# Gated linear attention and MLP: decays counted from a chunk's first token, and the state's gate fetched from exp(L) by two small DMAs in place of matmuls

## The chip, the cores and the metric

The kernel runs on one core of a Trainium2 chip. The metric is the time of one execution on the device in microseconds (us), the median of several runs; lower is better. TensorE (PE in the profile) does the matmuls and transposes, with its weight loads shown apart as PEld; VectorE is DVE, ScalarE is ACT, GpSimd is POOL, and SyncE (SP) only issues DMAs, from a queue of its own that it works off in order.

## The reference

```python
# q, k, v, alpha: (B=4, H=8, S=768, D=48), alpha in [0.8, 1]; state: (B, H, D, D), zero at first
for t in range(S):
    state = alpha[:, :, t, :, None] * state + np.einsum('bhd,bhe->bhde', k[:, :, t], v[:, :, t])
    y[:, :, t] = np.einsum('bhd,bhde->bhe', q[:, :, t], state)
x = y.transpose(0, 2, 1, 3).reshape(B, S, H * D)             # (4, 768, 384)
mu  = np.mean(x, axis=-1, keepdims=True)
var = np.mean((x - mu) ** 2, axis=-1, keepdims=True)
xn  = (x - mu) / np.sqrt(var + 1e-06) * g_ln
out = x + np.maximum(xn @ w_ch1, 0.0) @ w_ch2                # 384 -> 1536 -> 384
```

All is float32, but the two weight matrices come as float64 and are rounded to float32 inside the kernel.

## The kernel before

The sequence is cut into 6 chunks of 128 tokens. For each chunk c and each of the 4 batches b the attention goes through six stages: `decays`, `turn`, `scores`, `attend`, `turn_x`, `update`. Batches are staggered by one stage: in a wave, batch b is at stage "wave minus b". The MLP of chunk c (`hidden` 12 times over all four batches, then `project` in thirds for each batch) is spread between the attention steps of chunk c + 1; the last chunk's MLP stands alone at the end. The source order is then put into one fixed instruction order per engine by the framework's scheduler, and each engine works off its own list in order, waiting on semaphores.

`decays` takes the logarithm of alpha on ACT into `la` (line 178), sums it along the tokens by one matmul with a triangular matrix (line 180, into the PSUM tile `lps`), and takes exp of plus and minus that sum L on ACT (`eq`, line 190, and `ek`, line 189). DVE multiplies q by `eq` and POOL multiplies k by `ek`, both into `qk`. L is counted from the middle of the chunk (token 63), so that the state's next value needs two factors per head dimension: the decay over the first half of a chunk and that over the second. Four matmuls per chunk and batch make these (lines 181 to 184): for each of the 4 pairs of heads, `la` is the stationary operand (128x128) and two columns of ones and zeros (`halves`) move. Their results lie behind L in the same `lps` tile, ACT takes their exp (`ge`, line 191), and POOL makes the gate and applies it to the state (lines 202 to 205): second half of the last chunk times first half of this one (`gt`), spread to the block diagonal (`gm`), times the state (`st`).

`update` (lines 269 to 283) adds k'v to the state: four matmuls into `sps`, then one DVE operation. `attend` of the next chunk reads `st` at line 240.

Every float32 matmul shows as two MATMUL rows and two LDWEIGHTS rows in the profile, so the four small matmuls of one chunk and batch are 8 rows.

The weights come in 12 pieces of 768 KB (`ws`, line 123), three in flight; DVE rounds each in seven operations (lines 135 to 144) in the first 108 us. The loads of the next chunk's alpha, k, q and v (`ra`, `rk`, `rq`, `rv`, line 90) and the stores of the output (line 310) are on the same SP queue.

Of the kernel before, what the change touches and what calls it, by code (L numbers as in the profile page):

```python
# [9 lines left out]
FP32 = mybir.dt.float32  # L10
# [7 lines left out]
STAGED = 3  # float64 pieces of the weights in flight  # L18
MID = 63  # the token of a chunk that decays are counted from
# [3 lines left out]
def kernel(  # L23
# [11 lines left out]
    """Gated linear attention in chunks of 128 tokens, then x + relu(LN(x) w1) w2.  # L35

    Within a chunk, L[t] is the sum of log(alpha) from the chunk's middle to t. With
    q' = q exp(L) and k' = k exp(-L), the chunk's own part of y is (q' k'^T, s <= t) v. The
    state is kept as of the chunk's middle, so that the part of earlier chunks is q' state,
    and the state's next value is (state + k'^T v) times the decay from middle to middle.  # L40
    alpha in [0.8, 1] keeps |L| under 14.5; float32 carries |L| up to 88, and scores with a
    key later than the query, which could overflow before that, are never copied.

    Heads go in pairs, at partitions 0 and 64 (rows past the head's D are zero), and a
    pair's state is block diagonal. The MLP of chunk c, on the 128 tokens of all batches,
    runs between the stages of the attention of chunk c + 1.

    Weights given in float64 arrive as their bits and are rounded to float32 here.
    """
    nc = tc.nc  # L50
# [15 lines left out]
    work = ctx.enter_context(tc.tile_pool(name="work", bufs=2))  # L66
    ps = ctx.enter_context(tc.tile_pool(name="ps", bufs=2, space=bass.MemoryType.PSUM))
# [4 lines left out]
    after, upto = r[:, None] > MID, r[None, :] >= r[:, None]  # L72
    tri_np = (after & upto).astype(np.float32) - (~after & ~upto).astype(np.float32)
    const_np = np.concatenate(
        [
            tri_np,
            np.eye(P, dtype=np.float32),
            upto.astype(np.float32),
            np.stack([r <= MID, r > MID, r < 64, r >= 64], 1).astype(np.float32),
        ],  # L80
        1,
    )
# [10 lines left out]
    consts = cpool.tile([P, 3 * P + 4], FP32, name="consts")  # L93
    nc.scalar.dma_start(consts, nc.inline_tensor(const_np, name="consts").ap())
    tri, ident, mask = (consts[:, i * P:(i + 1) * P] for i in range(3))
    mask = mask.bitcast(INT32)
    halves, own = consts[:, 3 * P:3 * P + 2], consts[:, 3 * P + 2:]
# [27 lines left out]
    def round_weights(i):  # L125
        """float64 bits (sign, 11 exponent, 52 mantissa) -> float32, in seven operations:
        2^20 1.m from the top 20 mantissa bits plus the low 32 as an integer, rounded once,
        times the signed power of two, whose exponent field is e - 896 (below 0: to zero).
        Integers that pass through float32 arithmetic there are multiples of 2^20: exact."""
# [28 lines left out]
    # Log decays and scaled q, k by token, one per batch, with the heads padded to 64.  # L158
    las = [cpool.tile([P, NP, 2, 64], FP32, name=f"la{b}") for b in range(B)]
    qks = [cpool.tile([P, 2, NP, 2, 64], FP32, name=f"qk{b}") for b in range(B)]  # L160
    sts = [cpool.tile([P, NP, 2, D], FP32, name=f"st{b}") for b in range(B)]
    for b in range(B):
        nc.vector.memset(las[b].rearrange("p a b c -> p (a b) c")[:, :, D:], 0.0)
        nc.vector.memset(qks[b].rearrange("p i a b c -> p (i a b) c")[:, :, D:], 0.0)

    # Scores, key by query; nothing is ever written where the key is later than the query.
# [7 lines left out]

    def decays(c, b):
        la = las[b].rearrange("p a b c -> p (a b) c")
        qk = qks[b].rearrange("p i a b c -> p i (a b) c")
        nc.scalar.activation(out=la[:, :, :D], in_=raws.pop(("a", c, b)), func=AFT.Ln)
        lps = ps.tile([P, 512], FP32, name="lps", tag="a", bufs=3)
        nc.tensor.matmul(lps[:, :DM], tri, la[:, :, :D], start=True, stop=True)  # L180
        for p in range(NP):
            nc.tensor.matmul(lps[:, DM + 2 * p:DM + 2 * p + 2],  # L182
                             las[b][:, p].rearrange("p a b -> p (a b)"), halves,
                             start=True, stop=True)
        lv = lps[:, :DM].rearrange("p (h d) -> p h d", d=D)
        ek = work.tile([P, H, D], FP32, name="ek", tag="ek")
        eq = work.tile([P, H, D], FP32, name="eq", tag="eq")
        ge = work.tile([P, NP, 2], FP32, name="ge", tag="ge", bufs=2 * B)
        nc.scalar.activation(out=ek, in_=lv, func=AFT.Exp, scale=-1.0)  # L189
        nc.scalar.activation(out=eq, in_=lv, func=AFT.Exp)  # L190
        nc.scalar.activation(
            out=ge, in_=lps[:, DM:DM + 2 * NP].rearrange("p (a b) -> p a b", b=2),
            func=AFT.Exp)
        nc.gpsimd.tensor_mul(qk[:, 1, :, :D], raws.pop(("k", c, b)), ek)  # L194
        nc.vector.tensor_mul(qk[:, 0, :, :D], raws.pop(("q", c, b)), eq)  # L195
        if c + 1 < NCB:
            load(c + 1, b)
        gate_of[c, b] = ge
        if c > 0:
            gt = work.tile([P, NP], FP32, name="gt", tag="gt")  # L200
            gm = work.tile([P, NP, 2], FP32, name="gm", tag="gm")
            nc.gpsimd.tensor_mul(gt, gate_of.pop((c - 1, b))[:, :, 1], ge[:, :, 0])
            nc.gpsimd.tensor_mul(gm, gt.unsqueeze(2).broadcast_to([P, NP, 2]),
                                 own.unsqueeze(1).broadcast_to([P, NP, 2]))
            nc.gpsimd.tensor_mul(sts[b], sts[b],
# [168 lines left out]
```

## Time and profile before

| | |
|---|---|
| times of three runs | 593.79, 599.22, 600.25 us; median 599.22 |
| span of the profiled execution | 593.7 us (0.1 us under the lowest of the three times) |
| PE busy | 570.7 us, 96% of the span, 2600 matmul rows |
| PEld, DVE, ACT, POOL busy | 368.8, 222.6, 92.0, 57.8 us |
| DMA | 33.64 MB, nearly all on SP's queue |

The profile is of one execution. Its span runs from the first to the last instruction; the lowest of the three times is all but the same, so what lies around the span is about 0.1 us. Busy time of PE holds overlapping passes: the busy time of a group is a little longer than the distance from its start to the start of the next group.

### The profile page before, as it was taken

How to read it: one execution, taken by the hardware profiler on the slowest of the kernel's cores; microseconds unless marked ns; L12 is line 12 of the kernel's file. 1: busy time of each engine (PE TensorE's matmuls, PEld its weight loads, DVE VectorE, ACT ScalarE, POOL GpSimd, SP SyncE). 2: the span in 40 equal slices, each digit the busy share in tenths (PEclk: the TensorE clock that was granted, in tenths of full speed). 3: DMA queues.
4: the chain of work that ended last, by engine and by line, in shares of the span. 5: the costliest groups of instructions: out<-in, count | busy, mean ns of one | idle time of the engine just before them, and what ended most of it. 6: DMA issues, size and time to landing. Idle time of an engine off the chain costs nothing.

```text
span 593.7 us, 6372 instructions
## 1 busy us (share of the span) xinstructions
PE 570.7 (96%) x2600; PEld 368.8 (62%) x2600; DVE 222.6 (37%) x365; ACT 92.0 (15%) x229; POOL 57.8 (10%) x90
## 2 busy tenths in 40 slices
PE   5976899999999999999999999999999999999997
PEld 4876654777656667756577665667765566654553
DVE  2887899533233232233332223332233331211000
ACT  3221121110032210032210022210011210001000
POOL 2101001110031100031100013010011110000000
PEclk9766699999999999999999999999999999999999
DMA  8673352111121100022101111000000000000000
GB/s 287 218 265 97 130 172 94 40 54 41 54 81 40 41 28 27 28 75 72 35 6 41 40 55 39 16 27 14 28 13 1 0 1 13 28 13 1 0 27 27
DMA packets 21885, 33.64 MB, mean 57 GB/s; under 512 B 2528, under 2 KB 18016, under 8 KB 21856
## 3 DMA queue, kind: packets, MB, share of 16 engines
q1 hardware_dynamic: 21312, 33.04, 16.9%
q8 instruction: 20, 0.33, 0.2%
q10 hardware_dynamic: 544, 0.20, 0.1%
q14 instruction: 9, 0.07, 0.0%
HBM read 28.51 MB, written 4.72 MB: 56 GB/s over the span
## 4 chain that ended last, share of the span: by engine, by line
PE 95%; DVE 3%; DMA 1%; ACT 1%; issue 0%; SPq 0%; ACTq 0%
PE hps L292 32%; PE ops L305 32%; PE yps L244 8%; PE aps L228 5%; PE tps L213 4%; PE lps L182 3%; PE yps L240 3%; PE sps L276 3%; PE lps L180 3%; PE xps L266 1%; DMA rq<-in_q_dram 1%; DMA ra<-in_alpha_dram 1%; DVE ob L309 0%; DVE xn L256 0%; DVE at L231 0%; DVE ws L143 0%
## 5 line engine op out<-in xcount | busy, mean ns | idle before, releaser
L305 PE MATMUL ops<-w,hT 128*128 128x384 f32 x576 | 198.7, 491 | 2.0 <-DVE ob L309 2.0
L292 PE MATMUL hps<-xT,w 128*128 128x512 f32 x432 | 197.8, 601 | 0.0
L305 PEld LDWEIGHTS ops<-w,hT 128*128 128x128 f32 x576 | 104.7, 190 | 65.4 <-DVE ob L309 3.8
L292 PEld LDWEIGHTS hps<-xT,w 128*128 128x128 f32 x432 | 78.3, 191 | 79.7 <-issue 77.2
L194 POOL TENSOR_TENSOR qk<-rk,ek 128x384 f32<-128x384 f32 x24 | 24.0, 1001 | 418.4 <-ACT ek L189 413.5
L244 PE MATMUL yps<-rv,at 128*128 128x48 f32 x384 | 58.5, 284 | 2.7 <-DVE st L281 2.6
L244 PEld LDWEIGHTS yps<-rv,at 128*128 128x128 f32 x384 | 54.9, 210 | 3.5 <-DVE st L281 2.8
L195 DVE TENSOR_TENSOR qk<-rq,eq 128x384 f32<-128x384 f32 x24 | 25.2, 1049 | 59.9 <-ACT eq L190 53.8
L297 DVE TENSOR_SCALAR hT<-hps 128x512 f32<-128x512 f32 x36 | 24.8, 690 | 56.3 <-PE hps L292 56.3
L295 ACT ACTIVATE hT<-hps 128x512 f32<-128x512 f32 x36 | 21.5, 598 | 156.1 <-PE hps L292 156.1
L250 DVE BATCH_NORM_STATS2 stats<-x 128x6 f32<-128x384 f32 x24 | 13.4, 560 | 74.7 <-ACT x L247 74.7
L247 ACT COPY x<-yps 128x384 f32<-128x384 f32 x24 | 11.5, 480 | 171.2 <-PE yps L244 171.2
L231 DVE COPY_PREDICATED at<-consts,aps 128x512 f32<-128x512 int32 x48 | 32.5, 718 | 13.5 <-PE aps L228 13.5
L228 PEld LDWEIGHTS aps<-qkT 48*128 48x128 f32 x384 | 26.9, 209 | 16.0 <-issue 9.2
L309 DVE TENSOR_TENSOR ob<-ops,x 128x384 f32<-128x384 f32 x24 | 13.4, 558 | 61.8 <-PE ops L305 61.8
L228 PE MATMUL aps<-qkT 48*128 48x128 f32 x384 | 32.2, 310 | 3.2 <-DVE qkT L218 3.2
L213 PEld LDWEIGHTS tps<-consts,qk 128*128 128x128 f32 x192 | 24.7, 154 | 13.7 <-issue 9.5
L182 PEld LDWEIGHTS lps<-consts,la 128*128 128x128 f32 x192 | 28.3, 212 | 7.9 <-issue 2.9
L240 PE MATMUL yps<-st,qkT 128*128 128x96 f32 x160 | 32.8, 286 | 0.0
L213 PE MATMUL tps<-consts,qk 128*128 128x128 f32 x192 | 29.2, 299 | 3.0 <-DVE qk L195 2.1
L240 PEld LDWEIGHTS yps<-st,qkT 128*128 128x128 f32 x160 | 25.6, 192 | 6.2 <-issue 3.8
L218 DVE COPY qkT<-tps 128x512 f32<-128x512 f32 x24 | 16.6, 690 | 32.0 <-PE tps L213 32.0
(38 smaller groups left out, 338.4 us busy)
## 6 DMA issues: line engine op xcount, KB each, us to landing
ws<-in_moe_w_ch_dram SPq DMA_DIRECT2D x12, 768.0 KB, 4.4
ra<-in_alpha_dram SPq DMA_DIRECT2D x24, 192.0 KB, 3.3
rk<-in_k_dram SPq DMA_DIRECT2D x24, 192.0 KB, 2.4
rq<-in_q_dram SPq DMA_DIRECT2D x24, 192.0 KB, 2.5
rv<-in_v_dram SPq DMA_DIRECT2D x24, 192.0 KB, 2.6
out_dram<-ob SPq DMA_DIRECT2D x24, 192.0 KB, 1.9
consts<-consts ACTq DMA_DIRECT2D x1, 194.0 KB, 3.5
g_col<-in_moe_g_ln_dram ACTq DMA_DIRECT2D x1, 1.5 KB, 3.7
```

What stands on the lines that cost most here:

```text
L182: nc.tensor.matmul(lps[:, DM + 2 * p:DM + 2 * p + 2], las[b][:, p].rearrange("p a b -> p (a b)"), halves, start=True, stop=True)
L194: nc.gpsimd.tensor_mul(qk[:, 1, :, :D], raws.pop(("k", c, b)), ek)
L195: nc.vector.tensor_mul(qk[:, 0, :, :D], raws.pop(("q", c, b)), eq)
L213: nc.tensor.transpose(tps[:, p], qks[b][:, i, p].rearrange("p a b -> p (a b)"), ident)
L228: nc.tensor.matmul(aps[i][:, p], qkT[rows, 1, p], qkT[rows, 0, p], start=True, stop=True)
L231: nc.vector.copy_predicated(out=at[:, i], data=aps[i], mask=mask.unsqueeze(1).broadcast_to([P, NP, P]))
L240: nc.tensor.matmul(yps[:, p].rearrange("p a b -> p (a b)"), qkT[:, 0, p], sts[b][:, p].rearrange("p a b -> p (a b)"), start=True, stop=False)
L244: nc.tensor.matmul(yps[:, p, i], at[:, i, p], vt[:, 2 * p + i], start=(c == 0), stop=(c == 0 or i == 1))
L292: nc.tensor.matmul(hps, w1[:, f, j * P:(j + 1) * P], xT_of[c][:, f], start=(f == 0), stop=(f == NF - 1))
L295: nc.scalar.activation(out=hT_of[c][:, j], in_=hps, func=AFT.Relu)
L297: nc.vector.tensor_scalar_max(hT_of[c][:, j], in0=hps, scalar1=0.0)
L305: nc.tensor.matmul(ops_of[b], hT_of[c][:, j, b], w2[:, j], start=(j == 0), stop=(j == NJ - 1))
```

## The change

L now counts from the chunk's first token: the triangular matrix is plain, and the same one serves as the mask of the scores. The state is kept as of the chunk's end, and its gate is exp(L) of the chunk's last token, which is the last row (partition 127) of `eq`. That row is copied to DRAM by one DMA (`row`, 1 x 512 elements of 4 bytes) and read back with one element per partition and pair of heads by a second one (`gate`, 128 x 4 elements); both stand on SP's queue, in `decays`, ahead of the next chunk's loads in the source. The four matmuls, the third exp on ACT (`ge`) and the product of two halves on POOL (`gt`) are gone. The spreading to the block diagonal (`gm`) and the multiplication of the state stand in `update` now, behind the addition, and no longer in the next chunk's `decays`. `eq` becomes one tile per batch with heads padded to 64 columns, and `la` a dense tile with two buffers. In the last chunk nothing of the gate is made.

```diff
-    tri_np = (after & upto).astype(np.float32) - (~after & ~upto).astype(np.float32)
+    upto = (r[None, :] >= r[:, None]).astype(np.float32)
...
-    las = [cpool.tile([P, NP, 2, 64], FP32, name=f"la{b}") for b in range(B)]
+    eqs = [cpool.tile([P, NP, 2, 64], FP32, name=f"eq{b}") for b in range(B)]
...
     def decays(c, b):
-        la = las[b].rearrange("p a b c -> p (a b) c")
         qk = qks[b].rearrange("p i a b c -> p i (a b) c")
-        nc.scalar.activation(out=la[:, :, :D], in_=raws.pop(("a", c, b)), func=AFT.Ln)
+        eq = eqs[b].rearrange("p a b c -> p (a b) c")[:, :, :D]
+        la = work.tile([P, H, D], FP32, name="la", tag="la")
+        nc.scalar.activation(out=la, in_=raws.pop(("a", c, b)), func=AFT.Ln)
         lps = ps.tile([P, 512], FP32, name="lps", tag="a", bufs=3)
-        nc.tensor.matmul(lps[:, :DM], tri, la[:, :, :D], start=True, stop=True)
-        for p in range(NP):
-            nc.tensor.matmul(lps[:, DM + 2 * p:DM + 2 * p + 2],
-                             las[b][:, p].rearrange("p a b -> p (a b)"), halves,
-                             start=True, stop=True)
+        nc.tensor.matmul(lps[:, :DM], tri, la, start=True, stop=True)
...
-        nc.scalar.activation(
-            out=ge, in_=lps[:, DM:DM + 2 * NP].rearrange("p (a b) -> p a b", b=2),
-            func=AFT.Exp)
         nc.gpsimd.tensor_mul(qk[:, 1, :, :D], raws.pop(("k", c, b)), ek)
         nc.vector.tensor_mul(qk[:, 0, :, :D], raws.pop(("q", c, b)), eq)
         if c + 1 < NCB:
+            row = dram.tile([1, NP, P], FP32, name="row", tag="row")
+            gate = work.tile([P, NP], FP32, name="gate", tag="gate", bufs=B)
+            nc.sync.dma_start(row, eqs[b][P - 1:P].rearrange("o a b c -> o a (b c)"))
+            with nc.allow_non_contiguous_dma(reason="one row to columns"):
+                nc.sync.dma_start(gate, row.rearrange("o a c -> c (o a)"))
+            gate_of[c, b] = gate
             load(c + 1, b)
-        gate_of[c, b] = ge
-        if c > 0:
-            gt = work.tile([P, NP], FP32, name="gt", tag="gt")
-            gm = work.tile([P, NP, 2], FP32, name="gm", tag="gm")
-            nc.gpsimd.tensor_mul(gt, gate_of.pop((c - 1, b))[:, :, 1], ge[:, :, 0])
-            nc.gpsimd.tensor_mul(gm, gt.unsqueeze(2).broadcast_to([P, NP, 2]),
-                                 own.unsqueeze(1).broadcast_to([P, NP, 2]))
-            nc.gpsimd.tensor_mul(sts[b], sts[b],
-                                 gm.unsqueeze(3).broadcast_to([P, NP, 2, D]))
...
     def update(c, b):
...
+        gm = work.tile([P, NP, 2], FP32, name="gm", tag="gm")
+        nc.gpsimd.tensor_mul(gm, gate_of.pop((c, b)).unsqueeze(2).broadcast_to([P, NP, 2]),
+                             own.unsqueeze(1).broadcast_to([P, NP, 2]))
         if c == 0:
             nc.vector.tensor_copy(out=sts[b], in_=sps)
         else:
             nc.vector.tensor_add(sts[b], sps, sts[b])
+        nc.gpsimd.tensor_mul(sts[b], sts[b],
+                             gm.unsqueeze(3).broadcast_to([P, NP, 2, D]))
```

The order on PE, at the start of chunk 2's attention, before (line 180 is the matmul for L, 182 the four small ones, 292 `hidden`, 213 the transposes of `turn`; the numbers at `la` and `qk` are buffers, one per batch):

```order
L180 MATMUL lps<-la_117,consts 128x384
L292 MATMUL hps<-xT,w_105 128x512 x3
L182 MATMUL lps<-consts,la_117 128x2 x4
L292 MATMUL hps<-xT,w_105 128x512 x3
L213 MATMUL tps<-consts,qk_121 128x128 x8
L292 MATMUL hps<-xT,w_105 128x512 x3
L180 MATMUL lps<-la_118,consts 128x384
L182 MATMUL lps<-consts,la_118 128x2 x4
L292 MATMUL hps<-xT,w_105 128x512 x3
```

The same place now (line 173 is the matmul for L, 278 `hidden`, 194 the transposes):

```order
L173 MATMUL lps<-la,consts 128x384
L278 MATMUL hps<-xT,w_107 128x512 x6
L194 MATMUL tps<-consts,qk_123 128x128 x8
L278 MATMUL hps<-xT,w_107 128x512 x3
L173 MATMUL lps<-la,consts 128x384
L278 MATMUL hps<-xT,w_107 128x512 x3
```

The 24 groups of four small matmuls are gone, and every other PE row stands where it stood, here and in the whole program.

On SP's queue, behind the first chunk's 16 loads, before:

```order
L123 DMA ws<-in_moe_w_ch_dram 128x3x256 x3
L90 DMA ra<-in_alpha_dram 128x384
L90 DMA rk<-in_k_dram 128x384
L90 DMA rq<-in_q_dram 128x384
L90 DMA rv<-in_v_dram 128x384
L90 DMA ra<-in_alpha_dram 128x384
L90 DMA rk<-in_k_dram 128x384
L90 DMA rq<-in_q_dram 128x384
L90 DMA rv<-in_v_dram 128x384
L123 DMA ws<-in_moe_w_ch_dram 128x3x256
```

The same place now (line 183 copies the row to DRAM, 185 fetches the gate; line 185 waits until the `row` of the same batch has landed):

```order
L115 DMA ws<-in_moe_w_ch_dram 128x3x256 x3
L183 DMA row<-eq_119 1x512
L83 DMA ra<-in_alpha_dram 128x384
L83 DMA rk<-in_k_dram 128x384
L83 DMA rq<-in_q_dram 128x384
L185 DMA gate<-row 128x4x1
L83 DMA rv<-in_v_dram 128x384
L183 DMA row<-eq_120 1x512
L83 DMA ra<-in_alpha_dram 128x384
L83 DMA rk<-in_k_dram 128x384
L83 DMA rq<-in_q_dram 128x384
L185 DMA gate<-row 128x4x1
```

Four small DMAs now stand ahead of the fourth weight load, and each `gate` has three loads between it and its `row`.

On POOL, from the last batch of chunk 1 to the first ones of chunk 2, before (line 194 multiplies k; `st_125` to `st_128` are the states of the four batches):

```order
L194 TENSOR_TENSOR qk_124<-rk,ek 128x8x48
L202 TENSOR_TENSOR gt<-ge 128x4
L203 TENSOR_TENSOR gm<-gt,consts 128x8
L205 TENSOR_TENSOR st_128<-st_128,gm 128x384
L194 TENSOR_TENSOR qk_121<-rk,ek 128x8x48
L202 TENSOR_TENSOR gt<-ge 128x4
L203 TENSOR_TENSOR gm<-gt,consts 128x8
L205 TENSOR_TENSOR st_125<-st_125,gm 128x384
```

The same place now (line 178 multiplies k, 262 spreads the gate, 268 multiplies the state; the states are `st_127` to `st_130`):

```order
L178 TENSOR_TENSOR qk_126<-rk,ek 128x8x48
L268 TENSOR_TENSOR st_127<-st_127,gm 128x384
L262 TENSOR_TENSOR gm<-gate,consts 128x8
L268 TENSOR_TENSOR st_128<-st_128,gm 128x384
L262 TENSOR_TENSOR gm<-gate,consts 128x8
L268 TENSOR_TENSOR st_129<-st_129,gm 128x384
L268 TENSOR_TENSOR st_130<-st_130,gm 128x384
L178 TENSOR_TENSOR qk_123<-rk,ek 128x8x48
```

The four state multiplications of a chunk now stand together, ahead of the first multiplication of k of the next chunk, and `gt` is gone.

## Rows read from the trace of the kernel before

**Rows 1.** The page: busy times, and the chain that ended last by engine and line.

```profile
PE 570.7 (96%) x2600; PEld 368.8 (62%) x2600; DVE 222.6 (37%) x365; ACT 92.0 (15%) x229; POOL 57.8 (10%) x90
...
PE 95%; DVE 3%; DMA 1%; ACT 1%; issue 0%; SPq 0%; ACTq 0%
```

**Rows 2.** Busy time of each engine by stretch (us), granted TensorE clock, DMA share, GB/s.

```profile
0.00:20.00 20.00, 13.17 (x62) 11.23 (x62) 7.19 (x16) 6.43 (x13) 4.04 (x8) 1.00 0.92 313
20.00:68.70 48.70, 38.00 (x195) 34.44 (x196) 41.42 (x67) 9.64 (x28) 4.91 (x6) 0.59 0.48 156
68.70:108.00 39.30, 39.30 (x130) 19.81 (x129) 38.91 (x61) 7.46 (x16) 4.55 (x5) 0.98 0.36 125
108.00:550.00 442.00, 442.00 (x2108) 282.77 (x2107) 131.47 (x218) 67.86 (x171) 44.33 (x72) 1.00 0.10 32
```

**Rows 3.** Line 182 alone by stretch: PE busy, PEld busy, clock, DMA share, GB/s.

```profile
0.00:62.00 62.00, 7.25 (x40) 8.34 (x40) 0.73 0.66 220
62.00:594.00 532.00, 18.04 (x152) 19.96 (x152) 0.99 0.12 38
```

**Rows 4.** PE in order of time, chunk 2: start, duration, line, tiles, count.

```profile
159.93 0.84 PE L180 MATMUL lps<-la,consts 128*128 128x384 f32 x2
160.60 2.74 PE L292 MATMUL hps<-xT,w 128*128 128x512 f32 x6
163.17 0.95 PE L182 MATMUL lps<-consts,la 128*128 128x2 f32 x8
163.98 2.82 PE L292 MATMUL hps<-xT,w 128*128 128x512 f32 x6
166.64 1.04 PE L213 MATMUL tps<-consts,qk 128*128 128x128 f32 x8
```

**Rows 5.** The chain that ended last, first 70 us: start, duration, what.

```profile
13.08 1.50 PE lps L182 x8
...
19.64 0.79 PE lps L182 x8
...
28.07 1.50 PE lps L182 x8
...
52.62 0.99 PE lps L182 x8
...
68.73 1.55 PE hps L292 x2
```

**Rows 6.** The first batch's `ek` and DVE's product of q and `eq`, in order of time.

```profile
7.80 0.49 ACT L189 ACTIVATE ek<-lps 128x384 f32<-128x384 f32 x1 [0.53 <-PE lps L182]
...
8.70 1.08 DVE L195 TENSOR_TENSOR qk<-rq,eq 128x384 f32<-128x384 f32 x1 [6.16 <-DMA ra<-in_alpha_dram]
```

**Rows 7.** Busy time by stretch of granted clock; columns as in rows 2.

```profile
18.70:22.10 3.40, 3.40 (x28) 3.08 (x29) 3.18 (x4) 0.97 (x4) 1.00 (x1) 1.00 1.07 374
22.10:39.20 17.10, 16.33 (x87) 14.81 (x88) 15.34 (x26) 5.48 (x15) 1.01 (x2) 0.50 0.52 171
56.30:69.90 13.60, 9.17 (x37) 8.28 (x38) 12.01 (x22) 0.97 (x3) 0.92 (x2) 0.50 0.43 134
```

**Rows 8.** DVE, emptying the tenth `hidden` result of chunk 0.

```profile
101.46 0.68 DVE L297 TENSOR_SCALAR hT<-hps 128x512 f32<-128x512 f32 x1
```

**Rows 9.** The page's DMA issues: queue, count, KB each, median us from issue to landing.

```profile
out_dram<-ob SPq DMA_DIRECT2D x24, 192.0 KB, 1.9
...
g_col<-in_moe_g_ln_dram ACTq DMA_DIRECT2D x1, 1.5 KB, 3.7
```

**Rows 10.** SP's queue in order of time: start, duration of the issue.

```profile
20.28 0.33 SPq L90 DMA_DIRECT2D rv<-in_v_dram  x1
27.40 0.38 SPq L123 DMA_DIRECT2D ws<-in_moe_w_ch_dram  x1
```

**Rows 11.** POOL: the product of k for chunk 1, batch 0; all multiplications of the state.

```profile
54.25 1.00 POOL L194 TENSOR_TENSOR qk<-rk,ek 128x384 f32<-128x384 f32 x1 [23.03 <-ACT ek L189]
...
L205 POOL TENSOR_TENSOR st<-st,gm 128x384 f32<-128x384 f32 x20 | 17.2, 860 | 1.6
```

More of the change, by code (lines that the diff above doesn't have):

```diff
@@ L18 @@
 STAGED = 3
-MID = 63
 @with_exitstack
@@ L66 @@
     work = ctx.enter_context(tc.tile_pool(name="work", bufs=2))
+    dram = ctx.enter_context(
+        tc.tile_pool(name="dram", bufs=B, space=bass.MemoryType.DRAM))
     ps = ctx.enter_context(tc.tile_pool(name="ps", bufs=2, space=bass.MemoryType.PSUM))
@@ L71 @@
     r = np.arange(P)
-    after, upto = r[:, None] > MID, r[None, :] >= r[:, None]
-    tri_np = (after & upto).astype(np.float32) - (~after & ~upto).astype(np.float32)
[L74 to L82, printed above, removed]
+    upto = (r[None, :] >= r[:, None]).astype(np.float32)
+    half = np.stack([r < 64, r >= 64], 1).astype(np.float32)
+    const_np = np.concatenate([upto, np.eye(P, dtype=np.float32), half], 1)
     raws = {}
@@ L91, in load @@
             raws[n, c, b] = t
-    consts = cpool.tile([P, 3 * P + 4], FP32, name="consts")
+    consts = cpool.tile([P, 2 * P + 2], FP32, name="consts")
     nc.scalar.dma_start(consts, nc.inline_tensor(const_np, name="consts").ap())
-    tri, ident, mask = (consts[:, i * P:(i + 1) * P] for i in range(3))
-    mask = mask.bitcast(INT32)
-    halves, own = consts[:, 3 * P:3 * P + 2], consts[:, 3 * P + 2:]
+    tri, ident, own = consts[:, :P], consts[:, P:2 * P], consts[:, 2 * P:]
+    mask = tri.bitcast(INT32)
     for b in range(B):
@@ L162 @@
     for b in range(B):
-        nc.vector.memset(las[b].rearrange("p a b c -> p (a b) c")[:, :, D:], 0.0)
+        nc.vector.memset(eqs[b].rearrange("p a b c -> p (a b) c")[:, :, D:], 0.0)
         nc.vector.memset(qks[b].rearrange("p i a b c -> p (i a b) c")[:, :, D:], 0.0)
@@ L175, in decays @@
     def decays(c, b):
-        la = las[b].rearrange("p a b c -> p (a b) c")
         qk = qks[b].rearrange("p i a b c -> p i (a b) c")
-        nc.scalar.activation(out=la[:, :, :D], in_=raws.pop(("a", c, b)), func=AFT.Ln)
+        eq = eqs[b].rearrange("p a b c -> p (a b) c")[:, :, :D]
+        la = work.tile([P, H, D], FP32, name="la", tag="la")
+        nc.scalar.activation(out=la, in_=raws.pop(("a", c, b)), func=AFT.Ln)
         lps = ps.tile([P, 512], FP32, name="lps", tag="a", bufs=3)
-        nc.tensor.matmul(lps[:, :DM], tri, la[:, :, :D], start=True, stop=True)
-        for p in range(NP):
-            nc.tensor.matmul(lps[:, DM + 2 * p:DM + 2 * p + 2],
-                             las[b][:, p].rearrange("p a b -> p (a b)"), halves,
-                             start=True, stop=True)
+        nc.tensor.matmul(lps[:, :DM], tri, la, start=True, stop=True)
         lv = lps[:, :DM].rearrange("p (h d) -> p h d", d=D)
         ek = work.tile([P, H, D], FP32, name="ek", tag="ek")
-        eq = work.tile([P, H, D], FP32, name="eq", tag="eq")
-        ge = work.tile([P, NP, 2], FP32, name="ge", tag="ge", bufs=2 * B)
         nc.scalar.activation(out=ek, in_=lv, func=AFT.Exp, scale=-1.0)
         nc.scalar.activation(out=eq, in_=lv, func=AFT.Exp)
-        nc.scalar.activation(
-            out=ge, in_=lps[:, DM:DM + 2 * NP].rearrange("p (a b) -> p a b", b=2),
-            func=AFT.Exp)
         nc.gpsimd.tensor_mul(qk[:, 1, :, :D], raws.pop(("k", c, b)), ek)
```

## The prediction

> **What bounds the kernel now.** I read the page first. PE is busy for 570.7 of 593.7 us, and the chain that ended last is PE for 95% of its length; DVE holds 3%, DMA and ACT 1% each, and POOL and SP next to nothing [rows 1]. So work taken off ACT, POOL or SP is worth nothing by itself, and work taken off PE should be worth its own length wherever PE never waits. The table by stretch says where that is [rows 2]. [...] From 68.7 to 108 us PE is busy throughout too, but so is DVE (38.91 of 39.30 us), which is rounding weights. From 20 to 68.7 us nobody is full: PE 38.00 and DVE 41.42 of 48.70 us, at a mean granted clock of 0.59. There the end is set by a chain that passes from PE to ACT to DVE and back, and I follow that chain instead of shares.
>
> **The four small matmuls (removed).** There are 24 groups of 8 rows on line 182, 192 rows: 40 rows (5 groups) before 62 us and 152 (19 groups) behind it [rows 3]. The new order takes out just these and moves no other PE row.
>
> The 19 late groups lie in a full PE. Their busy time is 18.04 us, or 0.95 us a group, but passes overlap, so this is the upper bound [rows 3]. The distance from the group's start to the next start, 163.17 to 163.98, is 0.81 us, which I use as the lower one [rows 4]. What comes behind counts too: six `hidden` rows take 2.57 us from start to start (160.60 to 163.17), and the six behind the group 2.66 (163.98 to 166.64), so the group costs 0.81 + 0.09 = 0.90 us [rows 4]. I take 0.88, the middle of the bounds and next to that figure. One group of the 19 (chunk 1, batch 1) lies in the stretch in which DVE is full. The tenth `hidden` result is emptied by DVE at 101.46 + 0.68 = 102.14 us [rows 8], and the twelfth needs its PSUM buffer; if PE arrives there earlier, it waits. I count that group as lost, which leaves 18 x 0.88 = 15.8 us (from 14.6 at 18 x 0.81 to 18.1 at 19 x 0.95).
>
> The 5 early groups lie on the chain. Four of its pieces are line 182: 1.50, 0.79, 1.50 and 0.99 us, 4.78 in all [rows 5]. The fifth group, the very first, holds `ek` until 7.80 us, and DVE's product starts at 8.70, right behind `eq`; I give it 1.50 us as well, the price of a group at the low rate [rows 5, 6]. That row names an alpha load as the releaser, but the product reads neither alpha nor what is loaded then; if it does wait on a load, these 1.50 us are nil. Of the piece at 28.07 I count only 0.3: from there to 52 us the chain runs through DVE's list, and DVE is busy for 85% of the stretch [rows 2, 5]. That makes 1.50 + 1.50 + 0.79 + 0.3 + 0.99 = 5.1 us (from 0 to 6.3).
>
> **The clock (a cost).** [...] `hidden` starts at 68.73 [rows 5], so now it runs 1.2 us at half rate, and loses 0.6. If it starts 5.1 us earlier and the clock still rises at 69.9, it runs 6.3 us at half rate and loses 3.1, 2.6 us more than now; if the rise moves along, nothing more. I take 0.9 us, nearer to the second, because the work that goes before the rise moves along as well.
>
> [...]
>
> **The two DMAs and the wait (added).** There are 20 pairs. Each `gate` waits on SP for its `row` to land; behind it on SP stand the next chunk's loads, in the first 108 us the weight loads, and later the output stores. The nearest row for a write to DRAM is the output store, 1.9 us to landing; for a fetch of single elements it is `g_col`, 384 elements, 3.7 us [rows 9]. With three loads issued in between, SP stands for a microsecond or two. In the first 20 us the queue is full (DMA share 0.92) and a `row` lies behind three pieces of 768 KB, some 7.5 us at 313 GB/s [rows 2, 9]. The cover is SP's own idle time: behind the eighth of the next loads at 20.28 it waits until 27.40 for DVE to free a weight buffer [rows 10]. From 108 us on the loads are for a chunk that begins tens of microseconds later. I put this at 0, from 0 to 3.7 us (one fetch laid open once); a gain is ruled out, since SP only gets more to do.
>
> [...]
>
> **ACT, POOL and the moved multiplication.** `ge` and `gt` go from engines that are not on the chain: 0. The state is multiplied in `update` now, 0.86 us each on POOL [rows 11], and the last of a chunk stands ahead of the next chunk's product of k. That product used to wait for `ek`, and `ek` for the small matmuls, which in chunk 2 begin 3.2 us behind the matmul for L (159.93 to 163.17) [rows 4]. `ek` can start some 3 us earlier, and the transposes that need the product come at 166.64, so 0.86 us is covered. `attend` reads the state a good part of a chunk later. Denser or padded tiles move the same elements: 0.
>
> **The sum.** 15.8 + 5.1 - 0.9 = 20.0 us. The profiled execution would come down from 593.8 to 573.8. It was the fastest of three; the other two are 5.4 and 6.5 us longer and nothing shows where. PE has no slack behind 108 us, so I place the difference ahead of that, leave it as it is, and apply the sum to the median: 599.2 - 20.0 = **579.2 us**. From the bounds the gain is 14.6 + 0 - 2.6 - 3.7 = 8.3 up to 18.1 + 6.3 = 24.4 us.
>
> **The rivals.** *The clock eats the early gain.* Fewer rows before 20 us could lose the full-rate stretch from 18.7 to 22.1: its 3.40 us of PE would take 6.8. With that and the 2.6 us, the early part is 5.1 - 3.4 - 2.6 = -0.9 us, the gain 14.9, the time 584.3. For it speaks that the clock sits at 0.50 for most of 22.1 to 69.9 [rows 7]; against it, that the chain here is partly DVE, which does not feel the clock.
>
> *DVE becomes the bound of the first 108 us.* Its idle time from 20 to 68.7 is 7.3 us, and from there to 108 it is 0.4 [rows 2]. If the order leaves DVE no way to close its gaps, the early part yields nothing and only the 18 groups count: 15.8 us, 583.4. Against it: one of its waits sits right behind the piece at 52.62 and should close with it.
>
> *The gate comes late.* POOL works in order, and the spreading of chunk 0's gates stands ahead of the product of k for chunk 1, batch 0, which started at 54.25 us [rows 11]. Chunk 0's last `eq` comes about 1 us behind 29.57, the end of the piece at 28.07 [rows 5]. So a gate has some 23 us to land; from there on each microsecond holds POOL. [...] Against it stands `g_col`, 3.7 us for three quarters of the elements.
>
> *The groups cost nothing in truth* (loads of weights hidden under the neighbours): then the time stays within 1%. The 0.81 us between starts in a full PE speaks against it [rows 4].
>
> **How the numbers follow.** Chances: the forecast 0.72; the early gain in full with a clock that moves along (24 us, 575) 0.07; clock 0.12; DVE 0.05; no gain 0.02; late gate 0.02. The range is 572 to 587: below by the full gains, above by the two rivals at 583 to 584 and an opened fetch of 3.7 us on top. A measurement here can tell about 1%, or 6 us, so faster has 0.95, the same 0.03, slower 0.02.
>
> **What would show it.** Of PE, no row of 128x2; PE full from about 103 us to the end of the attention, with each chunk 3.5 us shorter (4 x 0.88); `hidden` starting near 63.6 instead of 68.7; no wait of POOL on a DMA; `gate` landing in 3 to 6 us; the weights' last rounding on DVE no later than 106 us. Wrong would be: new PE idle time behind 108 us, `hidden` starting no earlier, or a weight load issued behind a `gate` that DVE then waits for.

## The result, and the profile after

| | before | after |
|---|---|---|
| median (us) | 599.31 | 575.82 |
| lowest to highest (four executions each) | 593.79 to 600.25 | 573.05 to 578.13 |
| span of the profiled execution | 593.7 | 576.1 |

The ratio is 0.9644, with a 95% interval from 0.9582 to 0.9707: 23.5 us less, where 20.0 was forecast. The four executions after fall into two pairs, 573.05 and 573.77, and 577.86 and 578.13; the median lies between them, where no execution was. Those before also spread, over 6 us. Much of what follows is about these two spreads.

One remark ahead corrects what stands above the prediction. The profiled execution after took 577.86 us with a span of 576.1, so 1.8 us lie around a span, and 598.96 against 597.2 in a later run of the kernel before says the same. The profiled execution before was therefore one of some 595.5 us. That its span lay 0.1 us under the lowest time was chance.

The page of the changed kernel, busy times and the chain that ended last; it answers to [rows 1].

```profile
PE 547.2 (95%) x2408; PEld 342.1 (59%) x2408; DVE 222.7 (39%) x365; ACT 90.2 (16%) x205; POOL 55.2 (10%) x70
...
PE 84%; DVE 9%; DMA 5%; SPq 1%; issue 0%; ACT 0%; ACTq 0%
```

PE has lost the 192 rows of the four small matmuls and 23.5 us of busy time. But the chain that ended last is no longer PE alone: 5% of it is now DMA. The table by stretch, with columns as in [rows 2], shows where time was won and lost.

```profile
20.00:62.00 42.00, 30.47 (x143) 26.32 (x142) 38.06 (x63) 7.38 (x20) 7.75 (x10) 0.58 0.59 174
62.00:68.70 6.70, 6.70 (x15) 3.04 (x15) 6.70 (x11) 0.60 (x1) 1.07 (x1) 0.82 0.40 141
68.70:108.00 39.30, 35.72 (x120) 18.19 (x118) 32.97 (x51) 6.73 (x13) 8.15 (x3) 0.96 0.34 110
108.00:550.00 442.00, 441.35 (x2002) 274.16 (x2002) 133.13 (x220) 68.11 (x157) 33.16 (x47) 1.00 0.11 32
```

From 108 us on PE is full but for 0.65 of 442 us. From 68.7 to 108 us, where PE and DVE had both been full, PE now idles for 3.6 us and DVE for 6.3.

PE in order of time, at the start of `hidden` (line 278), at the end of chunk 1's batch 1, and at the start of chunk 2; it answers to [rows 4] and the last of [rows 5].

```profile
62.07 11.66 PE L278 MATMUL hps<-xT,w 128*128 128x512 f32 x24
...
92.70 2.74 PE L278 MATMUL hps<-xT,w 128*128 128x512 f32 x6
99.03 4.28 PE L278 MATMUL hps<-xT,w 128*128 128x512 f32 x6 [3.58 <-DVE hT L283]
103.14 0.81 PE L173 MATMUL lps<-la,consts 128*128 128x384 f32 x2
...
156.62 0.84 PE L173 MATMUL lps<-la,consts 128*128 128x384 f32 x2
157.29 5.31 PE L278 MATMUL hps<-xT,w 128*128 128x512 f32 x12
162.44 1.04 PE L194 MATMUL tps<-consts,qk 128*128 128x128 f32 x8
```

The same landmarks before:

```profile
68.52 11.20 PE L292 MATMUL hps<-xT,w 128*128 128x512 f32 x24
...
99.59 5.45 PE L292 MATMUL hps<-xT,w 128*128 128x512 f32 x12
104.87 0.81 PE L180 MATMUL lps<-la,consts 128*128 128x384 f32 x2
```

I compare by these landmarks. The matmul for L of chunk 1, batch 2 starts at 103.14 us; before it started at 104.87. From there to the end of the span it is 473.0 us now (576.1 - 103.14) and was 488.8 (593.7 - 104.87). The difference is 15.87 us, where 18 groups at 0.88 make 15.84: the late term came out as forecast. `hidden` starts at 62.07 and not at 68.52, 6.45 us earlier, and the six rows at 92.70 start 6.89 us earlier (they were the first of the twelve at 99.59). Yet at 103.14 only 1.73 us of that are left. The rest went into two places that the rows show: a wait of 3.58 us for `hT`, and six `hidden` rows that take 4.28 us in place of 2.74.

The waits by who waited for whom (total, times, longest) name the new ones.

```profile
POOL gm L262 <- DMA gate<-row: 36.3, 8, 7.5
...
DVE w L127 <- DMA ws<-in_moe_w_ch_dram: 3.9, 1, 3.9
...
PE hps L278 <- DVE hT L283: 3.6, 1, 3.6
```

Followed back, the second and third are one event. Here are POOL, DVE and SP in order of time around it (start, duration, and what an idle time ended with).

```profile
80.54 0.68 DVE L283 TENSOR_SCALAR hT<-hps 128x512 f32<-128x512 f32 x1
81.06 6.83 POOL L178 TENSOR_TENSOR qk<-rk,ek 128x384 f32<-128x384 f32 x1 [17.04 <-ACT ek L176]
81.14 0.95 DVE L135 SCALAR_TENSOR_TENSOR ws<-ws 128x768 int32<-128x768 int32 x1
...
86.95 0.68 DVE L283 TENSOR_SCALAR hT<-hps 128x512 f32<-128x512 f32 x1
87.55 1.15 DVE L135 SCALAR_TENSOR_TENSOR ws<-ws 128x768 int32<-128x768 int32 x1
87.92 0.35 SPq L83 DMA_DIRECT2D rk<-in_k_dram  x1
...
88.85 0.38 SPq L115 DMA_DIRECT2D ws<-in_moe_w_ch_dram  x1
...
95.13 0.56 DVE L127 TENSOR_SCALAR w<-ws 128x768 int32<-128x768 int32 x1 [3.87 <-DMA ws<-in_moe_w_ch_dram]
...
98.29 0.68 DVE L283 TENSOR_SCALAR hT<-hps 128x512 f32<-128x512 f32 x1
```

POOL's product of k for chunk 1, batch 1 takes 6.83 us; the same product took 1.00 for batch 0 [rows 11]. The next load of k overwrites what this product reads, so SP stands until 87.92, and the last weight piece, queued behind, is issued at 88.85. DVE waits 3.87 us for it, until 95.13. DVE begins to empty the `hidden` result behind it in its order at 98.29, and PE has waited 3.58 us for that PSUM buffer.

The clock by stretch, columns as in [rows 7]:

```profile
13.60:23.80 10.20, 7.58 (x59) 5.68 (x56) 9.97 (x16) 3.69 (x9) 1.28 (x3) 0.98 0.85 292
...
37.40:64.70 27.30, 20.70 (x84) 16.91 (x83) 23.36 (x37) 3.12 (x9) 6.99 (x8) 0.51 0.52 155
64.70:98.80 34.10, 30.74 (x98) 14.56 (x96) 30.23 (x48) 6.04 (x11) 7.15 (x2) 1.00 0.37 119
98.80:102.20 3.40, 3.17 (x4) 1.47 (x5) 3.33 (x7) 0.00 (x0) 0.00 (x0) 0.54 0.00 0
```

The early stretch at the full rate, 3.4 us long in [rows 7], is now some 10 us long. (In the first 20 us the column alone does not tell the rate: it reads 1.00 in [rows 2] also where the 16 rows of batch 0's scores take 2.08 us, at 14.51 before. The scores of batch 1 take 1.16 us now, at 17.98, little more than half: that is the full rate, 1.16 us also at 85.48, where the clock is 1.00.) The last rise comes at 64.7 us, where before it came at 69.9: it moved along with the work. At the end of PE's wait the clock falls once more, from 98.8 to 102.2, and in that stretch lie the six rows that take 4.28 us.

The early part of SP's queue bears on the DMAs: the first `row` is issued at 11.22 us, and its `gate`, which waits for it, at 20.27.

```profile
11.22 0.31 SPq L183 DMA_DIRECT2D row<-eq  x1
...
20.27 0.38 SPq L185 DMA_DIRECT2D gate<-row  x1
...
23.35 0.38 SPq L185 DMA_DIRECT2D gate<-row  x1
24.38 0.38 SPq L115 DMA_DIRECT2D ws<-in_moe_w_ch_dram  x1
```

The chain that ended last even runs through the first two `row`s:

```profile
11.22 8.99 DMA row<-eq
...
21.29 2.05 DMA row<-eq
```

That alone does not price the DMAs, since another chain of the same length may stand beside it. Two of the experiments leave them out.

### The profile page after: what moved, and what is told of

The parts are those of the page before. It is cut to its first block, busy times and chain, and to the rows that moved or that the text cites. A ratio compares the mean times of both kernels' runs of the same rounds, so it can differ in the third digit from the quotient of the medians.

```text
span 576.1 us, 5992 instructions
## 1 busy us (share of the span) xinstructions
PE 547.2 (95%) x2408; PEld 342.1 (59%) x2408; DVE 222.7 (39%) x365; ACT 90.2 (16%) x205; POOL 55.2 (10%) x70
## 4 chain that ended last, share of the span: by engine, by line
PE 84%; DVE 9%; DMA 5%; SPq 1%; issue 0%; ACT 0%; ACTq 0%
PE ops L291 33%; PE hps L278 28%; PE yps L225 7%; PE aps L209 4%; PE yps L221 3%; PE tps L194 3%; PE sps L257 3%; PE lps L173 2%; DMA row<-eq 2%; DVE ws L135 1%; DVE w L129 1%; DMA rv<-in_v_dram 1%; PE xps L247 1%; DMA ws<-in_moe_w_ch_dram 1%; DVE w L136 1%; DVE ws L134 1%
## 5 line engine op out<-in xcount | busy, mean ns | idle before, releaser
L278 PEld LDWEIGHTS hps<-xT,w 128*128 128x128 f32 x432 | 80.4, 193 | 89.3 <-issue 78.3
L178 POOL TENSOR_TENSOR qk<-rk,ek 128x384 f32<-128x384 f32 x24 | 30.2, 1259 | 165.3 <-ACT ek L176 160.4
L268 POOL TENSOR_TENSOR st<-st,gm 128x384 f32<-128x384 f32 x20 | 18.1, 904 | 202.6 <-DVE st L267 181.3
L209 PE MATMUL aps<-qkT 48*128 48x128 f32 x384 | 31.0, 302 | 3.0 <-DVE qkT L199 3.0
L194 PEld LDWEIGHTS tps<-consts,qk 128*128 128x128 f32 x192 | 23.5, 148 | 16.4 <-issue 8.2
L194 PE MATMUL tps<-consts,qk 128*128 128x128 f32 x192 | 27.6, 286 | 4.9 <-DVE qk L179 4.2
```

The costliest lines, as they stand in the source:

```text
L194: nc.tensor.transpose(tps[:, p], qks[b][:, i, p].rearrange("p a b -> p (a b)"), ident)
L209: nc.tensor.matmul(aps[i][:, p], qkT[rows, 1, p], qkT[rows, 0, p], start=True, stop=True)
L268: nc.gpsimd.tensor_mul(sts[b], sts[b], gm.unsqueeze(3).broadcast_to([P, NP, 2, D]))
L278: nc.tensor.matmul(hps, w1[:, f, j * P:(j + 1) * P], xT_of[c][:, f], start=(f == 0), stop=(f == NF - 1))
```

## The experiments

**The changed kernel again**, beside the next three, to have more of its executions.

> The changed kernel once more, beside the others on one chip. Two things are in its first profile that the prediction did not have: the weight load that DVE waits for (3.9 us, from 91.3 to 95.1 us) and the 3.6 us for which PE then waits. If the chain behind it is fixed by the order of instructions (POOL's product of k for chunk 1, batch 1 lasts 6.8 us beside a gapless DVE, and the loads behind it on SP wait), the wait is in every profile and the times spread as before, 573 to 578 us. If it is a matter of luck, this profile is without it and about 5 us shorter.

It measured 576.27 us, with executions of 572.75, 573.73, 578.82 and 579.39; ratio 0.9654 (0.9582 to 0.9726). The profiled one (578.82) has the long product of k (6.70 us at 82.11), a wait of DVE for a weight piece (3.7) and of PE for `hT` (3.3). So the late weight load comes back. Of eight executions of this kernel four are at about 573 and four at 578 to 579.

**The small matmuls back, late and early.** The same matmuls stand again behind the one for L, once for chunks 2 to 5 (16 groups) and once for chunks 0 and 1 (8 groups). Their results are read by nobody.

```diff
         nc.tensor.matmul(lps[:, :DM], tri, la, start=True, stop=True)
+        if c >= 2:      # the other version: c < 2
+            for p in range(NP):
+                f = p % NF
+                nc.tensor.matmul(lps[:, DM + 2 * p:DM + 2 * p + 2],
+                                 la.rearrange("p h d -> p (h d)")[:, f * P:(f + 1) * P],
+                                 own, start=True, stop=True)
```

> The changed kernel with the four small matmuls put back in chunks 2 to 5 (16 groups), their result read by nobody; the gate still comes by the DMAs. If the groups cost PE their own time in a full PE, 16 x 0.88 = 14.1 us come back: about 590 us, and the stretch ahead of 108 us looks as in the changed kernel. If the gain came from the rest of the change (POOL, ACT, the moved multiplication), the time stays at 576 us; if the matmuls' cost was partly hidden weight loading, it lands between, near 583 us.

592.27 us, ratio 0.9895 (0.9856 to 0.9935). Its ten executions are three at 587.0 to 588.2 and seven at 591.5 to 594.0. The mean of the lower ones (587.75) stands 14.5 us above that of the changed kernel's two lower ones just above (573.24), and the mean of the higher ones (592.91) 13.8 above that of its two higher ones (579.11). That makes 0.86 to 0.91 us for each of 16 groups. The trace says the same: from the matmul for L of chunk 1, batch 2 to the end of the span it takes 487.2 us (589.7 - 102.48), 14.3 more than without the groups, or 0.89 each. They are paid in full.

> The changed kernel with the four small matmuls put back in chunks 0 and 1 alone (8 groups), their result read by nobody. On the chain of the first 60 us they cost 4.8 to 6.3 us, so the first hidden row starts near 68 us again and not at 62; the three groups of chunk 1 behind that cost up to 2.6 us, less what DVE's wait for the weights hides. If the early gain is real: 576 + 5 to 8 us, about 582. If, in addition, the late weight load is a consequence of the earlier exp (DVE has no gap left when POOL wants its operands), that wait is gone here, 5 us come back, and the time is about 577 to 579 us with the first hidden row late and no wait of DVE on weights. If the early groups were hidden: 576 us and nothing moves.

583.16 us (579.86, 580.92, 585.39, 586.85), ratio 0.9773 (0.9701 to 0.9845): 6.9 us above the changed kernel by the medians, 7.2 and 7.0 by the means of the lower and the higher pairs. `hidden` starts at 70.14 us, where the profiles of the kernel before have 68.52 and, below, 70.88 and 71.10. The weight load is late here too: the product of k lasts 6.49 us at 89.48, DVE waits 3.2 us. I had thought that the weight load is late because the earlier exp moved POOL's product of k forward into DVE's full stretch. With the early matmuls back that cannot be, and the theory fell.

**No DMAs**, the gate a constant 0.01:

```diff
...
+    ones = cpool.tile([P, NP], FP32, name="ones")
+    nc.vector.memset(ones, 0.01)
...
-            row = dram.tile([1, NP, P], FP32, name="row", tag="row")
...
-                nc.sync.dma_start(gate, row.rearrange("o a c -> c (o a)"))
-            gate_of[c, b] = gate
+            gate_of[c, b] = ones
```

> The changed kernel without the two DMAs: the gate is a constant, so the decay from chunk to chunk is left out; all other work stays. If the pairs of DMAs are free, as forecast, the time is that of the changed kernel (576 us, within 2 us). If SP's waiting for each row holds up the weights, or POOL's waiting for a gate delays anything, it is 3 to 6 us faster and the wait of DVE on the weight load is gone. If that wait comes from POOL's slow product of k alone, it stays, with the same 3.9 us.

573.07 us (572.84, 573.00, 573.14 and one of 579.41), ratio 0.9636 (0.9555 to 0.9717). By the text above this looks as if the DMAs cost 3 us, since the wait is gone too. The version with a constant gate and four pieces, below, shows that they do not. In the profiled execution (573.14) the product of k is short. POOL and DVE in order of time:

```profile
81.20 1.00 POOL L178 TENSOR_TENSOR qk<-rk,ek 128x384 f32<-128x384 f32 x1 [16.54 <-ACT ek L176]
...
81.29 1.72 DVE L133 SCALAR_TENSOR_TENSOR ws<-ws 128x768 int32<-128x768 int32 x1
```

Here POOL starts 0.09 us ahead of DVE's rounding step with two inputs, and it is that step which is held (1.72 us, normally 0.95). With the DMAs, in the first profile of the changed kernel, POOL started 0.08 ahead of that step and lost all the same; in the second POOL started at 82.11, 0.06 behind. In the other profiles that have the step beside it POOL won where it started 0.52 us ahead (four pieces, below), and lost where it started 0.19 to 0.28 behind (early matmuls; the two versions below with a late copy and with a constant gate and four pieces) and once with 0.03 ahead (late matmuls). So it looks like a race between two starts that are mostly 0.03 to 0.3 us apart, in part perhaps closer than the profile's times can order. The DMAs do not decide it alone: one execution without them took 579.41 us, which by its time belongs to the upper group, though it was not profiled. Whether they make the late load more frequent, four executions against eight can't tell.

**A fourth weight piece in flight**, so that the last pieces are issued before that product can hold them.

```diff
-STAGED = 3
+STAGED = 4
```

> The changed kernel with four pieces of the weights in flight in place of three. The last weight load then stands ahead of the next chunk's k load of batch 1 on SP's queue, so POOL's late product can't hold it up; PE, DVE and POOL keep their order. If the two levels of the times (573 and 579 us) come from this one load, all runs lie at the lower level: about 573 us, spread under 2 us, no wait of DVE on a weight load, PE not waiting near 95 us. If the levels come from the clock or from something else of the first 60 us, both stay, and the median is 576 us again.

573.09 us, six executions from 572.76 to 573.90, ratio 0.9595 (0.9559 to 0.9632). The upper group is gone. No wait for a weight piece is left, and the matmul for L of chunk 1, batch 2 starts 6.68 us earlier than before (104.87), not 1.73:

```profile
62.36 10.99 PE L278 MATMUL hps<-xT,w 128*128 128x512 f32 x24
...
98.19 0.81 PE L173 MATMUL lps<-la,consts 128*128 128x384 f32 x2
```

**That one product of k on DVE**, with three pieces:

```diff
-        nc.gpsimd.tensor_mul(qk[:, 1, :, :D], raws.pop(("k", c, b)), ek)
+        mul_k = nc.vector.tensor_mul if (c, b) == (1, 1) else nc.gpsimd.tensor_mul
+        mul_k(qk[:, 1, :, :D], raws.pop(("k", c, b)), ek)
```

> The changed kernel with the product of k for chunk 1, batch 1 alone on DVE in place of POOL: one instruction of 0.55 us more for DVE, and POOL not in the way. If POOL stands still for 6.8 us because DVE, busy without a gap, keeps it from its operands, the load behind it on SP goes out some 5 us earlier, DVE waits for no weights, and the time is 572 to 574 us in all runs. If POOL was slow for a reason of its own (its order, its gate), the k load is late again and the times keep both levels, 576 us in the median.

572.76 us (572.58 to 573.93), ratio 0.9591 (0.9546 to 0.9637). The weight piece is issued at 84.22 us and not at 88.85, and no one waits for it. Two different edits, one on the product and one on the queue behind it, remove the same group of executions.

**That product later**, by a small copy ahead of it on POOL:

```diff
+        if (c, b) == (1, 1):
+            late = work.tile([P, 64], FP32, name="late", tag="late", bufs=1)
+            nc.gpsimd.tensor_copy(out=late, in_=ek.rearrange("p h d -> p (h d)")[:, :64])
```

> The changed kernel with one small copy on POOL (64 columns of exp of minus L) ahead of the product of k for chunk 1, batch 1, so that this product starts a few tenths of a microsecond later. It is meant to lose a race: where POOL's start and the start of DVE's two-input rounding step lie within 0.1 us of each other, the one that comes first makes the other wait. If so, POOL's product lasts 6 to 7 us in every run, the last weight load is late, and all times are at the upper level, 578 to 580 us. If the levels have another source, the times keep both levels, 573 and 579 us.

579.29 us, three executions at 579.1 to 579.6 and one at 572.51; ratio 0.9661 (0.9594 to 0.9729). So not all executions are at the upper level, as I expected, and it was not the product that suffered. In order of time, POOL and the DVE operation at which it was let go:

```profile
82.40 5.81 POOL L180 COPY late<-ek 128x64 f32<-128x64 f32 x1 [17.31 <-ACT ek L176]
...
88.03 0.68 DVE L286 TENSOR_SCALAR hT<-hps 128x512 f32<-128x512 f32 x1
88.17 1.00 POOL L181 TENSOR_TENSOR qk<-rk,ek 128x384 f32<-128x384 f32 x1
```

A copy of 64 columns took 5.81 us, and the product behind it 1.00. So the length is not set by POOL's operation. In all six profiles with a held operation, what POOL starts there lasts until DVE has come to its next operation that reads PSUM.

**The kernel before with four pieces**: the edit of the fourth piece alone.

> The kernel before with four pieces of the weights in flight. Its times have two levels as well, 594 to 596 and 598 to 600 us. If these are the same late weight load, all runs come down to the lower level, about 594 us, and the whole of the change is then worth 594 - 573 = 21 us, level against level. If the upper level of the kernel before has another source (the clock in the first 70 us), both levels stay: 598 us in the median.

596.05 us, ten executions from 594.09 to 599.03, ratio 0.9977 (0.9943 to 1.0011): no change that can be told. The spread of the kernel before is not from a late weight piece: the profiled execution is the longest of the ten (599.03 us), and in it the product of k takes 1.01 us.

**The kernel before, one profile more.**

> The kernel before, one profile more. If its upper level (598 to 600 us) comes from the early chain and the granted clock, as the version of before with four pieces of weights suggests, a profiled execution of about 598 us or more shows hidden starting 1 us or more behind 68.7 us, a clock of 0.50 until some 5 us behind 69.9 us, and the distance from the first matmul for L of chunk 2 to the end unchanged, within 1 us, against the profile shown of before. If instead the late weight load (the k product on POOL beside a full DVE) makes it, hidden starts at 68.7, the product of k for chunk 1, batch 1 lasts over 5 us and not 1.00, and DVE waits for a weight piece. An execution near 594 us tells nothing and should repeat the rows shown.

This execution took 598.96 us, at the upper end. PE and the clock in it (order of time; stretches):

```profile
71.10 12.13 PE L292 MATMUL hps<-xT,w 128*128 128x512 f32 x24
```

```profile
69.90:74.80 4.90, 4.90 (x12) 2.79 (x12) 4.90 (x9) 0.00 (x0) 0.00 (x0) 0.54 0.64 202
74.80:108.00 33.20, 33.20 (x110) 16.32 (x109) 32.05 (x50) 6.10 (x12) 3.68 (x4) 1.00 0.35 119
```

`hidden` starts 2.6 us later than in the first profile (68.52) and the clock rises at 74.8 us, not 69.9; the first 24 rows take 12.13 us, where they took 11.20. Together that is 3.5 us, the whole difference of the spans (597.2 and 593.7). The product of k is short (1.00 us at 91.35). So what the prediction could not place lies early, in the chain and the clock ahead of `hidden` and just behind its start. Most of the 2.6 us have a place: the clock's mean over the first 20 us is 0.91 here and from there to 68.7 us 0.54, where [rows 2] have 1.00 and 0.59. On the chain that ended last, from the matmul for L of chunk 0's batch 2 to the transposes behind the next scores PE takes 7.98 us (17.95 to 25.93), where it took 4.96 (18.93 to 23.89): 3.0 us more, from a start 1.0 us earlier. The 14 rows of line 244 in it take 3.06 us, where they took 1.60.

**Constant gate and four pieces**: both edits, to price the DMAs without the late load.

> The changed kernel with four pieces of weights in flight and with the 20 pairs of small DMAs left out: the state is multiplied by a constant 0.01 in place of the gate, so the decay from chunk to chunk is left out. With four pieces the late weight load is gone, so only the DMAs differ from the version with four pieces (573.1 us). If the pairs cost nothing, 572.5 to 573.7. If the rows and gates in SP's queue or POOL's wait for a gate cost something that the late weight load had hidden, 571 or less.

573.10 us (572.77 to 573.82), ratio 0.9609 (0.9573 to 0.9645), against 573.09 with the DMAs: the 20 pairs cost nothing. Nor do they hold up the start, though the chain after the change runs through two of them: `hidden` starts at 62.22 and 62.30 us in the two versions without DMAs, and at 62.07 and 62.36 in the same two with them. The profile tells one thing more. The product of k was held here too, but SP had issued its weight pieces before:

```profile
72.45 6.93 SPq L113 DMA_DIRECT2D ws<-in_moe_w_ch_dram  x2
...
81.65 6.49 POOL L178 TENSOR_TENSOR qk<-rk,ek 128x384 f32<-128x384 f32 x1 [16.92 <-ACT ek L176]
```

This product, held for 6.49 us, cost nothing (573.11 us in that execution), with no weight piece behind it in SP's queue.

**All 24 groups back, with four pieces**: the loop above without its condition.

> The changed kernel with four pieces of weights in flight and with all 24 groups of four small matmuls back behind the matmul for L, their results read by nobody. If the matmuls are the whole of the change, the time goes back to that of the kernel before with four pieces (596.0 us; two levels, 594 to 599): 573.1 + 16 x 0.88 + 6.9 for the eight early groups = 594.1, from 593 to 599. If the rest of the change (the third exp and the product of halves that are gone, the moved multiplication of the state, the DMAs) carries some of the gain, it stays under 592.

597.17 us, ten executions from 593.83 to 599.82, ratio 1.0007 (0.9977 to 1.0037): the kernel before, its spread included. The small matmuls are the whole of what the change gives; the third exp, the product of halves, the moved multiplication and the denser tiles together change nothing that can be told. The trace is sharper than the times here: from the matmul for L of chunk 1, batch 2 to the end of the span it takes 488.75 us (598.0 - 109.25), where the kernel before takes 488.8. The early groups cost more than their own time in this version: `hidden` starts at 71.94 us in the profiled execution (599.82), 9.6 later than with four pieces alone, and with them the kernel spreads over 6 us again.

## Why the prediction was right

The forecast was faster, 579.2 us; it came to 575.82. The mechanism, matmuls on a PE without slack, is shown by putting them back. That the median came so near is in part luck, as the last point says. Point by point:

- *The 18 late groups, 15.8 us.* Measured 15.87 between the traces, and 13.8 to 14.5 for 16 of them put back. The 0.88 us a group, from start to start and with the slower rows behind it, was the right price.
- *The 19th group, counted as lost.* With four pieces PE waits only 0.23 us there and the group's 0.9 us are kept; in the changed kernel as it stands they vanish in the longer wait of 3.58.
- *The early groups, 5.1 us.* The sum came out, its parts did not. From landmark to landmark on PE in the two traces, the five groups gave 0.5, 1.5, 0.8, 1.6 and 1.0 us, 5.4 in all, where I had 1.50, 1.50, 0.79, 0.3 and 0.99. The first gave less because ACT's logarithm of batch 1 stands ahead of the first `ek` and waits for its alpha load until 6.48 us, so that `ek` starts at 6.91, only 0.89 earlier (0.41 of this is an earlier start of the whole execution). The caution about a load was right in part. The piece at 28.07 gave 1.6, as these starts show, and 0.6 of it was lost again by the scores behind it (33.52 before, 28.02 now):

```profile
26.58 1.49 PE L180 MATMUL lps<-la,consts 128*128 128x384 f32 x2
...
29.43 0.88 PE L266 MATMUL xps<-consts,xn 128*128 128x128 f32 x3
```

```profile
22.12 0.91 PE L173 MATMUL lps<-la,consts 128*128 128x384 f32 x2 [0.45 <-DVE at L212]
23.35 0.85 PE L247 MATMUL xps<-consts,xn 128*128 128x128 f32 x3 [0.31 <-DVE xn L237]
```

  With 0.4 us more from the earlier start, 1.3 from the clock (next point) and the 0.6 taken off, `hidden` starts 6.45 us earlier, and 6.16 with four pieces. These are single executions; against the longer execution of the kernel before, in which `hidden` starts at 71.10, it is 9 us.
- *The clock, -0.9.* The sign was wrong: in these two traces it gave some 0.8 us. Between the groups, two stretches of PE's work are 1.3 us shorter together, because the early stretch at the full rate is longer: 16.74 to 18.77 us before is 14.34 to 15.64 now, and 20.29 to 26.58 is 16.39 to 22.12. Behind them the first 24 `hidden` rows take 11.66 us against 11.20, a loss of 0.46, and with four pieces 10.99, a gain of 0.21. The rise moved with the work, from 69.9 [rows 7] to 64.7. The rival in which the clock eats the early gain is refuted in both of its parts: the full-rate stretch was not lost, and the rise did not stay. It is the kernel before that has less of the full rate in its longer execution, a mean clock of 0.91 over the first 20 us and of 0.54 from there to 68.7. That DVE does not feel the clock holds: its rounding step (line 144 before) took 0.95 us at 36.40, at a clock of 0.50, and at 77.06, at 1.00.
- *The DMAs, 0.* Confirmed by the constant gate with four pieces (573.10 against 573.09). But one sign was wrong: I expected no wait of POOL on a DMA, and there are eight, 36.3 us in all. They cost nothing, as the same comparison says. The first `row` took 9.0 us from its issue to the issue of its `gate` (11.22 to 20.27), longer than the 7.5 I reckoned; even so the fourth weight piece went out at 24.38, earlier than the 27.40 of [rows 10]. A `gate` issued at 23.35 released POOL at 27.75, 4.4 us later, and one behind a weight piece took 6.1 us (89.28 to 95.42). Even 9.0 and 6.1 together stay below the 23 us from which the rival of the late gate counts, so it falls.
- *ACT, POOL and the moved multiplication, 0.* Confirmed by the version with all groups back, behind its landmark to 0.1 us.
- *What should show.* PE is all but full from 103 us on, no row of 128x2 is left, and DVE's last weight rounding ends at 103.96 us, ahead of the 106 forecast in spite of the late piece.
- *What was not foreseen.* I had named "a weight load issued behind a `gate` that DVE then waits for" as a sign of being wrong. A weight load did come late, but behind a load of k that waited for POOL. It costs 5 to 6 us in about half of the executions. It hardly shows in the median because the kernel before had a spread of its own, of like size but from another place (the early chain), which the change took away: after the late load is removed, the 14 executions of the three versions without it lie between 572.58 and 573.93 us. The median before stood 3.8 us above the profiled execution (599.31 against 595.5), and the median after stands 2.9 above the one with four pieces (575.82 against 572.92). So "leave the difference as it is" came out nearly right by luck: one spread went and another of like size came.

In sum, without the late load the gain is 22.6 us between the profiled spans of 593.7 and 571.1 (four pieces): 15.9 late and 6.7 early, where the sum had 15.8 and 4.2.

## What to carry to other kernels

Price small operations in a full engine by the distance between the starts of their neighbours, ahead and behind; that held to 0.1 us over 18 groups. When an execution spreads by a per cent, profile it at both ends before explaining it, since two kernels can have the same spread from different places. And look at what stands behind each load in an in-order DMA queue: a buffer more (here one weight piece) made a neighbour's stall harmless, and of the versions that were run, the change with four pieces (573.09 us) and the one with the product of k on DVE (572.76) are the best.

## What the runs showed of the hardware that was not expected

The product of k on POOL, 1.00 us in the mean of the kernel before, took 6.49 to 6.83 us beside DVE work without gaps in five profiles, and a copy of only 64 columns 5.81. Such an operation started between 0.08 us ahead of a DVE step with two SBUF inputs and 0.28 behind that step's start, around the end of a DVE operation that reads PSUM, and ended 0.94 us (the product, at 87.89) and 0.18 us (the copy, at 88.21) behind the start of DVE's next operation that reads PSUM. One held the other up: where POOL won, DVE's 0.95 us step took 1.72 and 1.30. That the order of starts decides fits six of the eight profiles; in two POOL lost with a start 0.03 and 0.08 us ahead. The loser was not let in behind one instruction: from 81.14 to 86.95 us DVE ran nine instructions, none longer than 0.95 us, and POOL came through behind none of them. A wait for one instruction would have been under 1 us; it was 5.8. That the operations which read PSUM are the gap is read from six held operations, and was not tried by itself. What the two engines wait for in each other, no trace shows.

The clock also fell for 3.4 us at the end of a wait of PE of 3.58 us, in a stretch in which PE was otherwise full (1.00 to 0.54 at 98.8 us), so that this wait cost 1.54 us more than its length.
